# Row maxima from half sums and half differences: differences in two banks of their own, half sums from the query stage on, and six query buffers with reloads

## The chip, the cores and the metric

The kernel runs on one core of one Trainium2 chip, in one launch. The metric is the device time of that core in microseconds (us); the value compared is the median over runs. Engine names: PE is the matrix engine (TensorE), DVE is VectorE, ACT is ScalarE, POOL is GpSimd, SP is SyncE, which issues most DMAs here.

## What is computed

```python
B, S, D, H = 1, 2048, 512, 32;  Dh = D // H          # 16
# A: sliding window of 8 keys, dilated by 2, its own q, k, v for 32 heads
qkv = x @ wqkv;  logits over idx = pos - (0, 2, ..., 14);  a = softmax(...) applied to v, @ wo_a
# B: 32 query heads share one key and one value head, all 2048 keys
q = (x @ wq).reshape(B, S, H, Dh).transpose(0, 2, 1, 3);  k = x @ wk;  v = x @ wv
p = softmax(einsum("bhqd,bkd->bhqk", q, k) * Dh ** -0.5)
b = einsum("bhqk,bkd->bhqd", p, v), heads joined, @ wo_b
g = sigmoid((x * gate_w).sum(-1))
out = g * a + (1 - g) * b
```

All inputs and outputs are fp32. The weights wq and wk of B are large enough that its softmax needs the maximum of each row.

## The kernel before

**The work of B** is cut into `NU` = 32 units, each of 512 queries by 4 heads. For a unit the program does two things. First it finds the maximum of each query over all 2048 keys: matmuls with the queries as weights (`max_mm`, L321) put scores of 128 queries by 512 keys into a PSUM bank, and DVE reduces them. Such a piece, one bank of 512 columns, is called a half here; a unit has 64 of them, all units 2048 (`NF`). Two rows of the query buffer (rows 62 and 63 of each row half) then receive the shifts worked out from the maxima (`shift_a` to `shift_d`). Later come 16 exponential steps per unit, 512 in all: in each, `exp_pair` (L470, L472) puts scores of 128 keys by 512 queries into the banks `eb` twice, ACT takes the exponential of 1024 columns, and `weighted` (L480) multiplies with the values into the bank `po`.

**Maxima** are formed in three ways. `fill_pair` reduces two halves in one DVE instruction from the two-bank tile `m2` (L341); `fill_one` reduces one half from the bank `m1`, in the front from `po` too (L352). The third way takes two key blocks together: max(a, b) = (a + b) / 2 + |a - b| / 2. `half_keys` forms the half sums and half differences of the keys once (`kcd`); then `fill_diff` multiplies the queries with the half differences into both banks of `m2`, ACT writes the absolute values to SBUF (`dd`, L416), and `fill_sum` multiplies with the half sums into `m1` and `po`, where one DVE instruction adds the absolute values and takes the maximum (L426). Such a group of two differences and two sums stands for four halves. `slots` is the list of what is still to be done, in order of units.

**The order** is written out by a program that keeps a clock for each engine (`clk`, `after`, with fixed costs such as T_R, T_LAT, T_TTR) and a time at which each bank is free (`free`). In the front (about the first 280 us) `stream` puts out the projection matmuls, 64 rows at a time: one half of the array rows takes a projection matmul, and the other row half either the next one or a single matmul of the maxima. The projections are 16 query blocks (`("q", m)`, the first two ahead of the stream) and 64 blocks of A (`("a", gg, j)`), called lumps, 24 matmuls each, which alternate between `eb[0]` and `eb[1]` (L1046); after each lump ACT copies its banks out and POOL adds the two row halves. Half sums are formed at lumps `("a", 0, 4)` and `("a", 0, 6)`.

In the steps, each iteration asks `fill_ready` for a pair on `m2` and for a single on `m1`. Singles are asked for only while

```python
return 2 * max(0, 16 * (NU - 1) - 16 - s) + PER_ROW * max(0, NJ - 4 - outs) < to_go()
```

holds. Three times, `out_phase` stops the steps and projects four blocks of 128 output rows, again by `stream`, with groups of half sums beside the projection (L735). A phase begins when the maxima are fewer than `LEAD` = 3 units ahead of the steps, or at a set step. The last four output rows are spread over the last steps (`spread`). POOL works at A's window attention from the front until the last third.

**Buffers.** `qst` has eight query buffers, the last two being halves of the tile `q67`. A unit's queries are loaded once, by `stack` (four DMAs on SP: L290, L291), into the buffer that `home` gives, and stay there from the maxima to the end of the unit's steps. `stack` is called in the query stage for the first eight units and then each time a unit's steps are over. `kcd` lies in a pool of the front; it is written to scratch and read back into `q67` (`half_back`) when those two buffers are no longer used.

## Time and profile before

| | |
|---|---|
| median of 3 runs | 1503.54 us (1503.17 to 1504.63) |
| the profiled execution | 1503.16 us, its span 1501.4 us |
| mean granted TensorE clock | 0.999 of full speed |
| busy of the span | PE 1477.8 us (98%), ACT 1284.1 (86%), DVE 1188.7 (79%), POOL 1023.6 (68%) |
| DMA | 87.75 MB, mean 58 GB/s |

The span runs from the first to the last instruction of the program; the time of an execution is 1.8 us more. In a group's row stand line, engine, operation, output<-input by the program's names (the bank tiles `m2`, `m1`, `po`, `eb` show as pm, ps, po, pe; queries in the two buffers of `q67` as q), the shape and the count, then after the bar the busy time in us, the mean of one instruction in ns, and the idle time of the engine just before, with what ended it. A row of a window gives its length, then the busy time and the count on each engine, the granted clock, the share of the DMA engines and GB/s. PE counts as busy while a matmul is in flight, so a busy PE is not PE at its peak.

### The profile page before, as it was taken

Reading aid. Unit: us, or ns where it says so; the run is one execution under the profiler, and the core shown is the slowest. Engines: PE = TensorE matmul, PEld = TensorE weight load, DVE = VectorE, ACT = ScalarE, POOL = GpSimd, SP = SyncE. Lnnn points to the kernel's source line nnn. Section 1 sums busy time; section 2 is a strip of 40 time slices with the busy share of each in tenths; the row PEclk is TensorE's granted clock in tenths of the full one; section 3 lists DMA queues with packets and bytes.
Section 4 is the critical chain, followed back from the end, with each engine's and each line's share of the span. In section 5 each row is a group of like instructions: output and inputs, shape, how many; then the busy total and the mean of one; then the engine's idle time right before and its main releaser. Section 6 shows DMA issues by size and latency. Waiting matters only on the chain.

```text
span 1501.4 us, 29244 instructions
## 1 busy us (share of the span) xinstructions
PE 1477.8 (98%) x10920; PEld 706.0 (47%) x10920; DVE 1188.7 (79%) x1813; ACT 1284.1 (86%) x1668; POOL 1023.6 (68%) x1804
## 2 busy tenths in 40 slices
PE   7999999999999999999999999999999999999998
PEld 4988888533333333333363334633333373333334
DVE  5976666788888888888888888888888878888801
ACT  4558988899999999999988999899999979999885
POOL 7866987788988888888898789888888030111020
PEclk9999999999999999999999999999999999999999
DMA  6754223121120211211202112021120000000000
GB/s 219 199 150 138 78 84 123 44 83 41 55 89 6 84 58 41 70 41 41 70 27 78 46 35 75 30 69 41 41 70 11 17 31 16 2 1 2 1 1 29
DMA packets 44287, 87.75 MB, mean 58 GB/s; under 512 B 9520, under 2 KB 25952, under 8 KB 39920
## 3 DMA queue, kind: packets, MB, share of 16 engines
q1 hardware_dynamic: 36704, 46.10, 10.2%
q0 software_dynamic: 6432, 37.94, 7.6%
q8 instruction: 86, 1.41, 0.4%
q10 hardware_dynamic: 1008, 1.84, 0.4%
q14 instruction: 57, 0.47, 0.1%
HBM read 59.02 MB, written 26.30 MB: 57 GB/s over the span
## 4 chain that ended last, share of the span: by engine, by line
PE 92%; ACT 4%; DVE 1%; issue 1%; POOL 1%; DMA 1%; DVEq 0%; ACTq 0%; POOLq 0%
PE po L480 33%; PE pe L470 25%; PE pm L321 8%; PE pe L1046 8%; PE ps L321 5%; PE pe L735 4%; PE pm L406 2%; ACT dd L416 2%; PE ps L406 1%; PE pe L180 1%; ACT pexp L472 1%; PE po L406 1%; PE ps L807 1%; PE pm L807 1%; DVE dd L426 0%
## 5 line engine op out<-in xcount | busy, mean ns | idle before, releaser
L472 ACT ACTIVATE pexp<-pe 128x1024 f32<-128x1024 f32 x1021 | 987.3, 1023 | 100.7 <-PE pe L470 98.0
L341 DVE TENSOR_REDUCE mx<-pm 128x2 f32<-128x1024 f32 x508 | 620.1, 1221 | 142.9 <-PE pm L321 138.9
L480 PE MATMUL po<-pexp,vst 128*32 128x512 f32 x4096 | 545.5, 605 | 0.0
L470 PE MATMUL pe<-qst,kst 64*128 64x512 f32 x1914 | 520.3, 454 | 3.6 <-ACT pexp L472 2.2
L470 PEld LDWEIGHTS pe<-qst,kst 64*128 64x128 f32 x1914 | 213.5, 184 | 421.5 <-ACT pexp L472 409.8
L352 DVE TENSOR_REDUCE mx<-ps 128x1 f32<-128x512 f32 x453 | 307.5, 679 | 3.3 <-PE ps L321 3.3
L321 PE MATMUL pm<-kst,qst 62*128 62x512 f32 x974 | 197.6, 397 | 1.4 <-DVE mx L341 1.4
L540 POOL TENSOR_TENSOR pr<-aext 128x256 f32<-128x256 f32 x256 | 182.8, 741 | 0.3
L321 PE MATMUL ps<-kst,qst 62*128 62x512 f32 x430 | 181.0, 421 | 0.7 <-DVE mx L426 0.4
L600 POOL TENSOR_TENSOR oa<-oa,av 128x256 f32<-128x256 f32 x224 | 164.4, 734 | 15.4
L480 PEld LDWEIGHTS po<-pexp,vst 128*32 128x32 f32 x4096 | 80.5, 108 | 174.1 <-issue 166.1
L597 POOL TENSOR_TENSOR av<-aext,lg 128x256 f32<-128x256 f32 x224 | 139.7, 623 | 12.6
L321 PEld LDWEIGHTS ps<-kst,qst 62*128 62x128 f32 x430 | 78.9, 184 | 72.4 <-DVE mx L352 67.1
L416 ACT ACTIVATE dd<-pm 128x512 f32<-128x512 f32 x166 | 92.2, 609 | 21.9 <-DVE mx L426 10.9
L1046 PE MATMUL pe<-wal,xh 64*128 64x384 f32 (+1 forms) x504 | 107.8, 337 | 0.0
L1046 PE MATMUL pe<-wah,xl 64*128 64x384 f32 (+1 forms) x504 | 107.7, 338 | 0.0
L1046 PE MATMUL pe<-wah,xh 64*128 64x384 f32 (+1 forms) x504 | 107.7, 338 | 0.0
L426 DVE CUSTOM_DVE_ANT_0 dd<-ps,dd 128x512 f32<-128x512 f32 x83 | 57.4, 692 | 58.9 <-PE ps L406 26.6
L321 PEld LDWEIGHTS pm<-kst,qst 62*128 62x128 f32 x974 | 93.9, 186 | 6.0 <-DVE mx L341 2.8
L506 POOL TENSOR_TENSOR rl<-rl,gate_t 128x16 f32<-128x16 f32 x31 | 6.9, 222 | 129.1 <-DVE rl L500 128.9
L546 POOL TENSOR_TENSOR tr<-pr 128x512 f32<-128x512 f32 x64 | 81.7, 1276 | 3.8
L256 POOL TENSOR_TENSOR stage<-stage,two 128x384 f32<-128x384 f32 x64 | 65.1, 1016 | 26.2 <-ACT two L247 13.4
(223 smaller groups left out, 1897.7 us busy)
## 6 DMA issues: line engine op xcount, KB each, us to landing
aext<-ad POOLq DMA_DIRECT2D x32, 1056.0 KB, 5.4
ad<-stage SPq DMA_DIRECT2D x32, 384.0 KB
qst<-qd SPq DMA_DIRECT2D x60, 128.0 KB
xraw<-xt SPq DMA_DIRECT2D x16, 256.0 KB
qd<-qhi SPq DMA_DIRECT2D x16, 256.0 KB
qd<-qlo SPq DMA_DIRECT2D x16, 256.0 KB
qst<-qd SPq DMA_DIRECT2D x60, 64.0 KB
qst<-ml SPq DMA_DIRECT2D x216, 2.0 KB
```

The lines of the kernel that those rows point to most:

```text
L321: nc.tensor.matmul(dst, qst[home(v)[0]][b:b + 62, pr, t * P:(t + 1) * P], kst[b:b + 62, kc * 512:(kc + 1) * 512], start=True, stop=True)
L341: nc.vector.tensor_reduce(m[:, :, pr, t, kc], dst, AX.X, ALU.max)
L352: nc.vector.tensor_reduce(m[:, odd, pr, t, kc:kc + 1], dst, AX.X, ALU.max)
L416: nc.scalar.activation(dd[0][:, odd], m2[:, odd, :], AF.Abs)
L470: nc.tensor.matmul(bank[:, odd, :], kst[b:b + 64, kt * P:(kt + 1) * P], qst[home(u)[0]][b:b + 64, pr, :], start=True, stop=True)
L472: nc.scalar.activation(e, bank, AF.Exp, scale=SCALE)
L480: nc.tensor.matmul(po[32 * i:32 * i + 32, :], vst[:, kt, :], pexp[s, i // 2][:, i % 2, :], start=(kt == 0), stop=(kt == NJ - 1))
L540: nc.gpsimd.tensor_mul(pr[:, k], q, e[:, o:o + NH, AC:2 * AC])
L546: nc.gpsimd.tensor_add(nx, cur[:, :, 0:n], cur[:, :, n:2 * n])
L597: nc.gpsimd.tensor_mul(av, e[:, o:o + NH, 2 * AC:].rearrange("p j (h d) -> p j h d", d=DH), lg[:, w].unsqueeze(3).to_broadcast([P, NH, AG, ...
L600: nc.gpsimd.tensor_add(ao, ao, av)
L1046: nc.tensor.matmul(front[2 if x == last else x % 2][0][:, b, :n], l[h], r[h], start=(i == 0), stop=(i == 3 * C - 1))
```

## The change

Four things change together.

- **Banks.** The two banks of `m2` become a pool that is released and allocated anew (`banks_of`): either one tile `m2` of two banks, as before, or two tiles `hv[0]` and `hv[1]` of one bank each. While `hv` is there, `fill_diff` puts out one difference matmul at a time, as a single of `stream`, into the bank of its row half, and the two banks come free separately. Up to three sums may be open (`pend`), and each of two `dd` buffers has its own times (`until`), so the next group's differences may go ahead of this group's sums. `hv` is there from the query stage to the last lump and in each output phase; in the steps `m2` is back.
- **Half sums earlier.** `half_sel` moves to lump `("q", 3)`, and `half_keys` to `("q", 4)` and `("q", 5)`, as soon as the banks are free (`wants`). From then on, while the next slots are paired, the front takes no direct reductions. `kcd` lies in the constant pool for good, so scratch `kd` and `half_back` go.
- **Six query buffers.** `load_next` loads the unit after the one whose maxima are being done, into any buffer that `vacant` gives: an empty one, one whose unit's steps are over, or one whose maxima are done and which is not to stay. Units that are at most `STAY` = 2 ahead of the steps when loaded stay until their steps are over. The others are loaded a second time by `load_again`, one or two units ahead of their steps.
- **Shifts through scratch.** For a unit that does not stay, `shift_d` writes its shifts to scratch `sd` in place of the query buffer, and `load_again` reads them back with two DMAs on SP.

Beside these, the value and gate columns of the first 16 lumps of A leave their bank in one ACT copy in place of two, unit 1 no longer shares its order of slots with unit 0, and `ended` (no new groups at the end of a stream) is set two to three items sooner. The core of the diff (small renamings left out; of `half_keys` and `half_parts` only the places of the tiles change):

```diff
@@ -34,7 +34,7 @@
-NB = 8
+NB, STAY = 6, 2
@@ -63,19 +63,32 @@
+    kcd = cp.tile([P, 2, 2, 512], F32R, name="kcd")
+    sd = dp.tile([NU, 2, 2, 1024], F32, name="sd")
...
-    m2 = pp.tile([P, 2, 512], F32, name="pm")
...
+    m2, hv, mp = None, [], []
+    def banks_of(two):
+        nonlocal m2
+        if mp:
+            mp.pop().release()
+        mp.append(tc.alloc_tile_pool(name="pair", bufs=1, space=PSUM))
+        m2, hv[:] = None, []
+        if two:
+            hv.extend(mp[0].tile([P, 512], F32, name=f"pd{x}") for x in range(2))
+            free["d0"] = free["d1"] = free["m2"]
+        else:
+            m2 = mp[0].tile([P, 2, 512], F32, name="pm")
+            free["m2"] = max(free["m2"], free["d0"], free["d1"])
+    free = {"m2": 0.0, "m1": 0.0, "e0": 0.0, "e1": 0.0, "po": 0.0, "d0": 0.0, "d1": 0.0}
+    banks_of(False)
@@ -278,31 +290,59 @@
-    stacked, asked = [], set()
-    def stack(u):
-        qb, hg = divmod(u, NHG)
+    there, where, holds, stayed, ended_max, outs_q, now_u = {}, {}, [None] * NB, set(), set(), [1], [0]
+    def vacant():
+        for k in sorted(range(NB), key=lambda k: -1 if holds[k] is None else holds[k]):
+            w = holds[k]
+            if w is None or w < now_u[0] or w in ended_max and w not in stayed:
+                return k
+    def load(v, k):
+        holds[k], where[v] = v, k
+        qb, hg = divmod(v, NHG)
...
-            dst = qst[home(u)[0]].rearrange("p c n -> p (c n)").bitcast(F32)
+            dst = qst[k].rearrange("p c n -> p (c n)").bitcast(F32)
...
-        stacked.append(clk["pe"] + 5.0)
+    def load_next(first=False):
+        v = len(there)
+        if first or v < NU and v <= (slots[0][0] if slots else NU) + 1 and v // 2 + (2 if outs_q[0] < 15 else 0) <= outs_q[0]:
+            k = vacant()
+            if k is not None:
+                if v - now_u[0] <= STAY:
+                    stayed.add(v)
+                load(v, k)
+                there[v] = clk["pe"] + 5.0
+    def load_again(w):
+        k = vacant()
+        if w in stored and k is not None:
+            load(w, k)
+            stayed.add(w)
+            for b in range(2):
+                nc.sync.dma_start(qst[k][64 * b + 62:64 * b + 64].rearrange("x i n -> x (i n)").bitcast(F32), sd[w, b])
+            shifted.add(w)
+    stored = set()
...
-    slots = [(v, pr, t, kc) for kc in range(2) for v in range(2) for pr in range(2) for t in range(4)]
-    slots += [(v, pr, t, kc) for v in range(2) for pr in range(2) for t in range(4) for kc in range(2, 4)]
-    slots += [(v, pr, t, kc) for v in range(2, NU) for pr in range(2) for t in range(4) for kc in range(4)]
+    slots = [(0, pr, t, kc) for g in range(2) for pr in range(2) for t in range(4) for kc in (2 * g, 2 * g + 1)]
+    slots += [(v, pr, t, kc) for v in range(1, NU) for pr in range(2) for t in range(4) for kc in range(4)]
...
     def fillable():
-        return bool(half) or bool(slots) and slots[0][0] < len(stacked) and stacked[slots[0][0]] <= clk["pe"]
+        return bool(half) or bool(slots) and there.get(slots[0][0], 1e9) <= clk["pe"]
@@ -372,60 +410,81 @@
+    def diff_ready():
+        if not group and (ended or half or not hv or not paired()):
+            return False
+        odd = group[0][4] if group else 0
+        now = clk["pe"]
+        return len(pend) < len(dd) + 1 and free[f"d{odd}"] <= now + 0.1 and dd[0][1][odd] <= now + 0.9 and clk["act"] <= now + 0.7 and clk["dve"] <= now + 1.8
...
     def fill_diff():
-        v, pr, t, kc = slots.pop(0)
-        slots.pop(0)
-        for odd in range(2):
-            half_mm(m2[:, odd, :], v, pr, t, kc, 1, odd)
-        at = after("pe", 0, T_R) + T_LAT
-        dd.append(dd.pop(0))
-        for odd in range(2):
-            nc.scalar.activation(dd[0][:, odd], m2[:, odd, :], AF.Abs)
-            ready_d[odd] = after("act", at, 0.52) + 0.1
-        free["m2"] = ready_d[1]
-        pend.extend([(v, pr, t, kc, 0), (v, pr, t, kc, 1)])
+        if not group:
+            v, pr, t, kc = slots.pop(0)
+            slots.pop(0)
+            group.extend([(v, pr, t, kc, 0), (v, pr, t, kc, 1)])
+        v, pr, t, kc, odd = group.pop(0)
+        dst, until = dd[0]
+        if odd:
+            dd.append(dd.pop(0))
+        half_mm(hv[odd], v, pr, t, kc, 1, odd)
+        at = clk["pe"] + T_R + T_LAT
+        nc.scalar.activation(dst[:, odd], hv[odd], AF.Abs)
+        at = after("act", max(at, until[odd]), 0.52) + 0.1
+        free[f"d{odd}"] = at
+        pend.append((v, pr, t, kc, odd, at, dst, until))
+    def sum_ready():
+        return pend and free[("m1", "po")[pend[0][4]]] <= clk["pe"] + 0.1 and pend[0][5] <= clk["pe"] + 0.4
...
     def fill_sum():
-        v, pr, t, kc, odd = pend.pop(0)
+        v, pr, t, kc, odd, ready, d, until = pend.pop(0)
...
-        nc.vector.tensor_tensor_reduce(dd[0][:, odd], dst, dd[0][:, odd], 1.0, -FMAX, ALU.add, ALU.max, m[:, odd, pr, t, kc:kc + 1])
-        free[key] = after("dve", max(clk["pe"] + T_R + T_LAT, ready_d[odd]), T_TTR) + 0.08
+        nc.vector.tensor_tensor_reduce(d[:, odd], dst, d[:, odd], 1.0, -FMAX, ALU.add, ALU.max, m[:, odd, pr, t, kc:kc + 1])
+        free[key] = until[odd] = after("dve", max(clk["pe"] + T_R + T_LAT, ready), T_TTR) + 0.08
...
+    def finish_groups():
+        while group or pend:
+            if group:
+                odd = group[0][4]
+                clk["pe"] = max(clk["pe"], free[f"d{odd}"])
+                fill_diff()
+            else:
+                odd, at = pend[0][4:6]
+                clk["pe"] = max(clk["pe"], free[("m1", "po")[odd]], at - 0.3)
+                fill_sum()
+            clk["pe"] += T_R
@@ -454,10 +513,13 @@
     def shift_d(v, ml, k):
...
-        dst = qst[home(v)[0]][64 * b + 62:64 * b + 64].rearrange("x i (t q) -> x i t q", t=4).bitcast(F32)
+        if v in stayed:
+            dst = qst[where[v]][64 * b + 62:64 * b + 64].rearrange("x i (t q) -> x i t q", t=4).bitcast(F32)
+        else:
+            dst = sd[v, b].rearrange("x (i t q) -> x i t q", i=2, t=4)
...
-            shifted.add(v)
+            (shifted if v in stayed else stored).add(v)
@@ -683,20 +745,24 @@
-    def stream(seq, mm, done, pooled):
+    def stream(seq, mm, done, pooled, held=()):
...
         while min(at) < len(seq):
...
-            if pend:
-                if free[("m1", "po")[pend[0][4]]] <= clk["pe"] + 0.1 and ready_d[pend[0][4]] <= clk["pe"] + 0.4:
-                    single, odd = fill_sum, pend[0][4]
-            elif paired() and not half:
+            if wants and all(free[k] <= clk["pe"] + 0.1 for k in (("m1", "po") if wants[0] else ("m2",))):
+                half_keys(wants.pop(0))
+            if sum_ready():
+                single, odd = fill_sum, pend[0][4]
+            elif hv and (group or paired() and not half):
+                if diff_ready():
+                    single, odd = fill_diff, group[0][4] if group else 0
+            elif 1 in wants:
...
-            elif fillable() and free["m1"] <= clk["pe"] + 0.1:
+            elif fillable() and not pend and free["m1"] <= clk["pe"] + 0.1:
...
-            elif pooled and fillable() and free["po"] <= clk["pe"] + 0.1:
+            elif pooled and fillable() and not pend and free["po"] <= clk["pe"] + 0.1:
@@ -704,16 +770,11 @@
-                elif at[b] < len(seq):
+                elif at[b] < len(seq) and not (seq[at[b]] in held and told < at[b]):
...
-            if ended:
-                pass
-            elif paired():
-                if not half and not pend and max(free["m2"], clk["dve"] - 1.2) <= clk["pe"] + 0.1:
-                    fill_diff()
-            elif slots and fillable() and free["m2"] <= clk["pe"] + 0.1:
+            if m2 is not None and not ended and 0 not in wants and slots and fillable() and free["m2"] <= clk["pe"] + 0.1:
@@ -756,17 +817,14 @@
-            formed.update((0, 1))
+            banks_of(True)
...
-        formed.clear()
+        finish_groups()
+        if whole_unit:
+            banks_of(False)
@@ -1034,10 +1092,16 @@
-            if lump == ("a", 0, 3):
+                dd.append((pm[0].tile([P, 2, 512], F32, name="dd", bufs=1), [0.0, 0.0]))
+            if lump == ("q", 3):
...
-            elif lump in (("a", 0, 4), ("a", 0, 6)):
-                half_keys(1 if lump[2] == 4 else 0)
+                dd.append((p1.tile([P, 2, 512], F32, name="dd", bufs=1), [0.0, 0.0]))
+            elif lump in (("q", 4), ("q", 5)):
+                wants.append(5 - lump[1])
+            elif x == last:
+                finish_groups()
+                banks_of(False)
+                front[2] = (m2, "m2")
@@ -1094,13 +1158,17 @@
-        if s == 16 * NB + 4:
-            half_back()
-        if len(stacked) < NU and s > 16 * (home(len(stacked))[1] + 1):
-            stack(len(stacked))
+        now_u[0] = u
+        if kt > 2:
+            for w in (u + 1, u + 2):
+                if w < NU and w in ended_max and w not in stayed:
+                    load_again(w)
+        load_next()
...
+                if u in stored:
+                    load_again(u)
```

90 lines of the change are left out of this document (38 added, 52 removed).

## The prediction

> **What bounds the kernel now.** I read the page first, then busy time by stage, the timeline of a few steps, and last the grouped instructions of the front (everything before the exponential steps, 0 to 282 us) and of what follows.
>
> ```profile
> span 1501.4 us, 29244 instructions
> PE 92%; ACT 4%; DVE 1%; issue 1%; POOL 1%; DMA 1%; DVEq 0%; ACTq 0%; POOLq 0%
> ```
>
> The chain that ended last is 92% PE, so a change pays only where it shortens PE's queue or lets a PE stall go. The stages differ:
>
> ```profile
> core 0: us, PE busy (x) PEld busy (x) DVE busy (x) ACT busy (x) POOL busy (x), PEclk, DMA share, GB/s
> 40.00:90.00 50.00, 50.00 (x449) 47.36 (x447) 49.93 (x67) 25.77 (x42) 42.65 (x43) 1.00 0.71 197
> 110.00:270.00 160.00, 156.38 (x1558) 140.58 (x1556) 105.64 (x328) 134.48 (x315) 128.86 (x205) 1.00 0.34 104
> 500.00:600.00 100.00, 100.00 (x699) 35.83 (x699) 86.88 (x105) 92.49 (x100) 87.07 (x171) 1.00 0.15 51
> 758.00:791.00 33.00, 32.52 (x288) 24.07 (x286) 27.68 (x80) 25.80 (x51) 28.48 (x50) 1.00 0.08 28
> ```
>
> The query projection (40:90) has a full VectorE and a half idle ScalarE; the projection of A (110:270) and an output phase (758:791) have room on both; the steps (500:600) have PE full and ScalarE at 92%. All work of this change is maxima: 2048 "halves" (128 queries by 512 keys). Where they are done today:
>
> ```profile
> L426 DVE CUSTOM_DVE_ANT_0 dd<-ps,dd 128x512 f32<-128x512 f32 x83 | 57.4, 692 | 58.9 <-PE ps L406 26.6 <-ACT dd L416 24.9 <-ACT mx L315 5.5
> L341 DVE TENSOR_REDUCE mx<-pm 128x2 f32<-128x1024 f32 x28 | 33.8, 1209 | 5.2 <-PE pm L321 5.2
> L352 DVE TENSOR_REDUCE mx<-ps 128x1 f32<-128x512 f32 x27 | 18.2, 674 | 2.8 <-PE ps L321 2.8
> L352 DVE TENSOR_REDUCE mx<-po 128x1 f32<-128x512 f32 x26 | 17.5, 674 | 0.0
> ...
> L341 DVE TENSOR_REDUCE mx<-pm 128x2 f32<-128x1024 f32 x480 | 586.3, 1221 | 137.7 <-PE pm L321 133.8
> L352 DVE TENSOR_REDUCE mx<-ps 128x1 f32<-128x512 f32 x426 | 289.3, 679 | 0.5 <-PE ps L321 0.5
> L426 DVE CUSTOM_DVE_ANT_0 pexp<-ps,pexp 128x512 f32<-128x512 f32 x53 | 36.7, 692 | 16.8 <-PE ps L406 12.0 <-ACT pexp L416 3.4 <-PE pe L735 1.2
> ```
>
> The first four rows are the front, the last three the rest. A group of half sums and differences is four halves (one L426 on each of ps and po, two halves each), so the front does 83 x 4 + 28 x 2 + 53 = 441, the steps 480 x 2 + 426, the output phases 53 x 4 = 212. The sum is 2039; a few records are missing.
>
> What one half costs PE is different in a step and in the front. A step with only a pair, then one with a pair and a single:
>
> ```profile
> 549.81 1.07 PE L480 MATMUL po<-pexp,vst 128*32 128x512 f32 x8
> 551.43 3.81 ACT L472 ACTIVATE pexp<-pe 128x1024 f32<-128x1024 f32 x4 [0.23 <-PE pe L470]
> 551.71 1.06 PE L480 MATMUL po<-pexp,vst 128*32 128x512 f32 x8
> 553.28 0.39 PE L321 MATMUL ps<-kst,qst 62*128 62x512 f32 x1
> 553.87 1.06 PE L480 MATMUL po<-pexp,vst 128*32 128x512 f32 x8
> ```
>
> ```profile
> 500.00:600.00 100.00, 50.08 (x376) 7.39 (x376) 1.00 0.15 51
> 500.00:600.00 100.00, 27.77 (x41) 1.00 0.15 51
> ```
>
> The second fence holds the windows of L480 (376 / 8 = 47 steps in 100 us) and of L352 (41 singles). The step from 549.81 to 551.71 had no single: 1.90 us. If the six others cost that, a step with a single costs (100 - 6 x 1.90) / 41 = 2.16 us. Nearly every step carries one, because the emitter asks for singles while more halves are left than pairs alone can do by step 480 (20 credited for each output row to come).
>
> In the front a half shares the array with the projection, in the other row half:
>
> ```profile
> 274.26 0.34 PE L1046 MATMUL pe<-wah,xl 64*128 64x384 f32 x2
> 274.44 0.34 PE L1046 MATMUL pe<-wah,xh 64*128 64x384 f32 x2
> 274.98 0.39 PE L406 MATMUL ps<-kcd,q 62*128 62x512 f32 x1
> 275.15 0.33 PE L1046 MATMUL pe<-wal,xh 64*128 64x384 f32 x1
> 275.21 0.34 PE L1046 MATMUL pe<-wah,xh 64*128 64x384 f32 x1
> ```
>
> Pairs of projection matmuls follow each other every 0.18 us (274.26, 274.44); the half at 274.98 holds its rows until 275.21, 0.23 us, while the other rows go on. A half costs PE 0.23 / 2 = 0.115 us there, against 2.16 - 1.90 = 0.26 us as a single.
>
> **The change part by part.**
>
> *Singles that leave the steps.* Taken away from one step in eight, a single is worth 0.26 us. Taken away from many in a row it is worth less, for ScalarE becomes the limit: its share of the 500:600 row is 92.49 / 47 = 1.97 us a step (saving 0.19); four exponentials back to back took 3.81 us, so two take 1.91 and with 0.03 for the rest 1.94 (saving 0.22). I take 0.21, ends 0.19 and 0.26. By the Trainium skill ("ScalarE: Activation LUTs", What ACT_TABLE_LOAD costs) an ACTIVATE takes 186 ns + 0.833 ns an element and back-to-back ones overlap by about 93 ns: an estimate of 0.95 us for 1024, in agreement with 3.81 / 4; by it the saving would be 0.24 and the time below some 4 us lower.
>
> *Front, query stage.* The half sums start some 50 us sooner, and the direct reductions there end. Between 40 and 90 us ScalarE has 24 us free; at 1.11 us a group (next fence) that is 22 groups, 88 halves, and I take 80. VectorE, full today, gives 86 in that stretch (its rows there: 21 pairs, 44 singles). So nothing is won: -6. The stretch around 90 to 110 us, where today the half sums are being formed, goes on at full rate: 7 lumps at 7 halves for 16 now, +33.
>
> *Front, projection of A.* Today's limit is the order difference, two |d|, two sums, then the next difference:
>
> ```profile
> L416 ACT ACTIVATE dd<-pm 128x512 f32<-128x512 f32 x156 | 86.7, 609 | 20.2 <-DVE mx L426 10.9 <-PE pm L406 9.1
> L246 ACT ACTIVATE stage<-pe 128x384 f32<-128x384 f32 x52 | 25.5, 490 | 4.9 <-PE pe L1046 2.2 <-DMA ad<-stage 1.6 <-PE po L406 0.3
> L426 DVE CUSTOM_DVE_ANT_0 dd<-ps,dd 128x512 f32<-128x512 f32 x78 | 54.0, 692 | 53.6 <-ACT dd L416 24.2 <-PE ps L406 22.0 <-ACT mx L315 5.5
> PEld pm L406 <- ACT dd L416: 13.0, 36, 1.6
> ```
>
> From 110 to 270 us: 52 lumps (L246 runs once in each), 3.08 us a lump, 78 groups, 1.5 a lump. ScalarE spends 86.7 / 78 = 1.11 us a group and (134.48 - 86.7) / 52 = 0.92 on the rest of a lump; VectorE 2 x 0.69 = 1.38 a group. PE waited 13.0 us for |d| to free the shared bank. Two banks, each freed by its own |d|, and two dd buffers let differences run ahead. The emitter charges ScalarE 0.8 + 1.04 g and PE 0.18 an iteration, 2.16 + 0.36 g a lump, and puts out a difference while its ScalarE clock is at most 0.7 us ahead: that closes at g = 2.0, less for the first 16 lumps (1.0 in place of 0.8), for gate copies and exponentials of A. I take 1.8, ends 1.5 and 2.0. On the chip PE then needs 12 x 0.175 + 7.2 x 0.115 = 2.93, ScalarE 0.92 + 1.8 x 1.11 = 2.92, VectorE 2.6: all under 3.08, but close together, so waits remain. Halves: 56 lumps x 0.3 x 4 = +67. Together the front gains 94. PE pays 94 x 0.115 = 10.8 us; I let half of the 13.0 us go and add 2 us for the two changes of banks and the tail of open groups before the last lump (0 to 4): front **+6** us, ends -5 and +20. What is late next is ScalarE: behind a difference that waits for its bank stand, on PE, the projection matmuls, and behind |d| on ScalarE the copies that free the projection's banks.
>
> *Output phases.* From one step's last matmul to the next:
>
> ```profile
> 756.39 1.06 PE L480 MATMUL po<-pexp,vst 128*32 128x512 f32 x8
> 793.41 1.06 PE L480 MATMUL po<-pexp,vst 128*32 128x512 f32 x8
> ```
>
> In such a phase of 37 us there are 53 / 3 = 18 groups. ScalarE has 33 - 25.8 = 7 us free, VectorE 5.3: four more groups (ends 0 and 7), 16 halves for 1.84 us of PE, and two bank changes with the wait for the last reader, between 0 and 1.4 us (|d| 0.61, then L426 0.69), taken as 0.7. Three phases: **+7.5** us, 48 halves.
>
> *Loads and shifts.* Six buffers for eight, units from the third on loaded twice, their shifts through scratch and back.
>
> ```profile
> 51.75 0.59 SPq L290 DMA_DIRECT2D qst<-qd  x1
> 53.62 0.58 SPq L291 DMA_DIRECT2D qst<-qd  x1
> SPq L458 <- POOL ml L444: 269.2, 18, 52.0
> ```
>
> A load is four issues from 51.75 to 54.2 us, 2.4 us of SP; a second load with its two shift reads about 3.6 us, some 29 times, 104 us of a queue that spends most of the span waiting. The load of a maxima unit is put out when the unit before it begins: 64 halves, some 10 lumps or 30 us ahead in the front, 22 steps or 47 us in the steps. That hides it; I cost it at nothing. On SP it can stand behind shift writes that wait for GpSimd (up to 52.0 us in the row); those waits end with the same GpSimd work as now, and mostly show SP idle, not late. If the cover went, each load would cost PE 2.4 us and a landing: 0 to 30 us over the whole kernel. Two ScalarE copies of 0.2 us become one in 16 lumps: off the path. DMA share 0.15 in the steps rises little.
>
> **Sum.** 94 + 48 = 142 singles x 0.21 = -29.8; front +6; phases +7.5: -16. From the profiled execution's own 1503.16 us (span 1501.4) that is 1487; the median of the runs shown is 0.4 us higher, so **1488**.
>
> **Rivals.**
>
> *B, no waits left.* ScalarE overlaps fully and 2.0 groups fit: PE 2.10 + 8 x 0.115 = 3.02 a lump, the front 4 us shorter, 187 halves gone from the steps at 0.23 = -43, phases +7.5: 1464. For it: every engine has room on average. Against: the waits of the last fence come from real times that differ from the charged ones, and those stay.
>
> *C, slower: the front becomes bound by emptying banks.* The emitter issues 2.0 groups a lump on charges that are too low (0.18 an iteration that holds a 0.23 us half; no charge for splits). Then a |d| follows its own difference without overlap, at 609 ns: ScalarE 0.92 + 4 x 0.609 = 3.36 a lump, and with today's PE wait of 13.0 / 78 = 0.17 a group, 3.70. Over 64 lumps +40; 187 halves save 39; phases +7.5: 1511. It decides from 3.57 us a lump on ((39 - 7.5) / 64 above 3.08). For it: ScalarE is already 84% busy from 110 to 270. Against: it has 25 us idle there and PE waits only 13. The Trainium skill ("TensorEngine Tiling (Array Packing)", PSUM Bottleneck) says that row tiling speeds up the array but not the emptying of PSUM, which may become the limit; by that rule C is what happens, and today's row (13.0 us in 160) bears it out only in part.
>
> *D, it hardly does what it says.* The emitter's own conditions (ScalarE 0.7 us, VectorE 1.8 us, open sums below three) hold the groups at 1.5 a lump and the phases at 18: the +33 and -6 halves stay, 27 x 0.21 = -6 against +3 in the front and +2 in the phases: 1503.
>
> **How the numbers follow.** The forecast has 0.62, B 0.12, C 0.17, D 0.09. About 0.2% (3 us) is what a measurement of this kernel can tell from no change. The forecast's own bounds (saving 0.19 to 0.26, front -5 to +20, groups 1.5 to 2.0) give 1470 to 1500. The range 1467 to 1508 adds the near side of B and D and the loads' price, and leaves out most of C. Faster is the forecast but a thin edge and B: 0.73. Same is D and that edge: 0.08. Slower is C and a small part of the rest: 0.19.
>
> **What would show it.** Right: L426 counts in the front near 105 to 125 a bank in place of 83; singles (L352 on ps) after the front near 280 to 290 in place of 426, gone in the second half of the steps, where steps last 1.92 to 1.97 us; the first L480 within 275 to 300 us; 20 to 24 groups a phase. Wrong: lumps above 3.5 us with PE waiting for ACT dd (C); single-free steps at 2.1 us; PE waiting for a load of qst or for shifts; L426 counts as now (D).

## The result: slower by 1.1%, and the profile after

The changed kernel took 1521.29 us (median of 4 runs, 1520.03 to 1522.22), the kernel before 1504.09 beside it (1503.17 to 1506.95): a ratio of 1.0111, 95% interval 1.0093 to 1.0128. The forecast was 1488, its range 1467 to 1508. The profiled execution took 1522.22 us. The head of its page, and the head of the chain that ended last:

```profile
span 1520.4 us, 29896 instructions
PE 1488.4 (98%) x10920; PEld 705.4 (46%) x10920; DVE 1145.3 (75%) x1847; ACT 1337.6 (88%) x1745; POOL 1013.4 (67%) x1793
PE 91%; ACT 4%; DVE 2%; DMA 1%; issue 1%; POOL 1%; SPq 0%; DVEq 0%; ACTq 0%; POOLq 0%
```

PE carries the chain as before, over 19.0 us more of span. The maxima moved as intended, which the VectorE groups show (front first, then the rest):

```profile
L473 DVE CUSTOM_DVE_ANT_0 dd<-ps,dd 128x512 f32<-128x512 f32 x122 | 84.2, 690 | 44.3 <-PE ps L440 19.0 <-ACT dd L460 13.3 <-PE pe L1110 4.4
L382 DVE TENSOR_REDUCE mx<-pm 128x2 f32<-128x1024 f32 x6 | 7.3, 1218 | 5.2 <-PE pm L361 5.2
L393 DVE TENSOR_REDUCE mx<-ps 128x1 f32<-128x512 f32 x8 | 5.5, 682 | 1.6 <-PE pe L1110 1.5
...
L382 DVE TENSOR_REDUCE mx<-pm 128x2 f32<-128x1024 f32 x469 | 572.6, 1221 | 168.6 <-PE pm L361 164.7
L393 DVE TENSOR_REDUCE mx<-ps 128x1 f32<-128x512 f32 x356 | 242.0, 680 | 1.4 <-PE ps L361 1.4
```

122 groups in the front where there were 83, and 356 singles after it where there were 426. (L440, L460 and L473 are the difference matmul, the |d| and the half sum, before L406, L416 and L426; L361, L382 and L393 are the score matmul, the pair and the single, before L321, L341 and L352.) Yet the front lasted longer than these groups save later. Cut at the first matmul of P times V, at step 480 and at the three output phases:

| us | before | after | difference |
|---|---|---|---|
| front, to the first PV matmul | 279.6 | 302.8 | +23.2 |
| halves done in it | 440 | 515 | +75 |
| three output phases | 109.6 | 114.4 | +4.8 |
| other steps to 480 | 1017.2 | 1010.1 | -7.1 |
| singles in the steps | 431 | 357 | -74 |
| after step 480 | 95.0 | 93.1 | -1.9 |

The loss is the front, and the gain of the steps is a quarter of the forecast's 29.8 us. In the windows of the changed kernel (query stage, projection of A, steps, output phase):

```profile
45.00:85.00 40.00, 39.08 (x321) 29.87 (x318) 23.78 (x62) 32.30 (x55) 31.42 (x30) 1.00 0.55 147
200.00:290.00 90.00, 90.00 (x892) 80.79 (x890) 72.80 (x221) 85.28 (x179) 75.55 (x117) 1.00 0.36 112
500.00:600.00 100.00, 100.00 (x701) 35.66 (x698) 87.24 (x107) 92.53 (x101) 83.73 (x154) 1.00 0.22 70
883.00:918.00 35.00, 34.98 (x304) 25.20 (x302) 30.20 (x87) 30.91 (x56) 33.00 (x50) 1.00 0.16 56
```

and the projection of A before, in the same columns:

```profile
180.00:270.00 90.00, 87.42 (x868) 77.82 (x868) 60.72 (x190) 74.57 (x164) 76.16 (x116) 1.00 0.31 96
```

PE's waits in the projection are gone (90.00 busy of 90, before 87.42), and ScalarE rose from 74.57 / 90 = 83% to 85.28 / 90 = 95%. Undisturbed lumps last 90 / 29 = 3.1 us, little more than before (90 / 30 = 3.0), with 53 / 29 = 1.83 groups in place of 46 / 30 = 1.53. So the front lost its time mainly elsewhere. Two stops of PE stand in its timeline; matmuls of 384 columns at 160.10 took 0.34 us, and then:

```profile
96.78 0.79 PE L440 MATMUL pd<-kcd,qst 62*128 62x512 f32 x1 [2.86 <-ACT dd L460]
...
160.10 0.34 PE L1110 MATMUL pe<-wah,xh 64*128 64x384 f32 x1
165.57 0.79 PE L440 MATMUL pd<-kcd,qst 62*128 62x512 f32 x1 [4.54 <-ACT dd L460]
167.55 0.52 PE L1110 MATMUL pe<-wah,xh 64*128 64x384 f32 x2
171.38 0.34 PE L1110 MATMUL pe<-wal,xh 64*128 64x384 f32 x1
```

The stops cost more than themselves, as the clock column of the windows around the second shows:

```profile
161.00:165.00 4.00, 0.04 (x2) 0.00 (x0) 0.00 (x0) 0.84 (x3) 0.00 (x0) 0.91 0.37 106
165.00:169.00 4.00, 3.43 (x20) 3.43 (x22) 2.10 (x6) 3.11 (x8) 1.70 (x2) 0.50 0.30 98
169.00:172.00 3.00, 3.00 (x26) 3.00 (x24) 1.02 (x3) 2.00 (x5) 2.54 (x3) 0.65 0.00 0
172.00:176.00 4.00, 4.00 (x40) 3.45 (x38) 3.04 (x11) 3.72 (x9) 2.90 (x4) 1.00 0.46 147
```

After the stop PE ran at a granted clock of 0.50 until 171.1 (the 0.65 of 169:172 is 2.1 us at half speed). Half the speed for 5.5 us loses 2.75, so the stop cost about 4.54 + 2.75 = 7.3 us; the first, with half speed from 96.8 to 102.8, cost 2.86 + 3.0 = 5.9. Both figures are estimates: they suppose that PE set the pace while its clock was low. The Trainium skill ("TensorE: Matmul & The Clock Gate", Part 1, The HAM clock gate) says that PE's clock goes to half after an idle window of about 3.4 us and comes back after as long a busy one. The trace agrees on the half, but not on an idle window: the clock fell at 96.0, 2.1 us after PE's last matmul, and the first stop was only 2.86 us long; it came back after 6.8 us both times.

What stopped PE at 161? Its difference waited for a bank, the bank for |d|, and |d| stood on ScalarE behind a copy (L258) that waited 4.83 us for its buffer, whose contents a store on SP had yet to take. SP's timeline and its wait:

```profile
157.72 0.40 SPq L275 DMA_DIRECT2D ad<-stage  x1
158.16 4.88 SPq L520 DMA_DIRECT2D qst<-ml  x7
164.12 14.82 SPq L275 DMA_DIRECT2D ad<-stage  x3
```

```profile
SPq L520 <- POOL ml L503: 8.3, 1, 8.3
```

L520 writes the shifts of a unit. SP had stood 8.3 us at the first (156.99) until GpSimd had formed ml; the store at 157.72 came right behind it, and the copy went on at 164.16, when it had landed. In the first stop |d| waited for its own place instead: the second dd buffer lies where the queries had been, and had to wait for a DMA that still read them (3.4 us).

### The profile page after: what moved, and what is told of

It is laid out like the page before. It is cut to its first block, busy times and chain, and to the rows that moved or that the text cites. A ratio compares the mean times of both kernels' runs of the same rounds, so it can differ in the third digit from the quotient of the medians.

```text
span 1520.4 us, 29896 instructions
## 1 busy us (share of the span) xinstructions
PE 1488.4 (98%) x10920; PEld 705.4 (46%) x10920; DVE 1145.3 (75%) x1847; ACT 1337.6 (88%) x1745; POOL 1013.4 (67%) x1793
## 4 chain that ended last, share of the span: by engine, by line
PE 91%; ACT 4%; DVE 2%; DMA 1%; issue 1%; POOL 1%; SPq 0%; DVEq 0%; ACTq 0%; POOLq 0%
PE po L542 32%; PE pe L532 24%; PE pe L1110 9%; PE pm L361 7%; PE ps L361 4%; PE pe L796 4%; PE pd L440 3%; PE ps L440 2%; PE po L440 2%; ACT pexp L534 2%; PE ps L865 1%; PE pm L865 1%; PE pe L193 1%; DMA ad<-stage 1%; DMA xraw<-xt 1%
## 5 line engine op out<-in xcount | busy, mean ns | idle before, releaser
L382 DVE TENSOR_REDUCE mx<-pm 128x2 f32<-128x1024 f32 x475 | 579.9, 1221 | 173.8 <-PE pm L361 169.9
L532 PE MATMUL pe<-qst,kst 64*128 64x512 f32 x2042 | 543.3, 458 | 4.4 <-ACT pexp L534 4.3
L393 DVE TENSOR_REDUCE mx<-ps 128x1 f32<-128x512 f32 x364 | 247.5, 680 | 3.0 <-PE pe L1110 1.5
L361 PE MATMUL pm<-kst,qst 62*128 62x512 f32 x953 | 191.8, 397 | 1.8 <-DVE mx L382 1.3
L662 POOL TENSOR_TENSOR oa<-oa,av 128x256 f32<-128x256 f32 x224 | 164.0, 732 | 14.7
L460 ACT ACTIVATE dd<-pd 128x512 f32<-128x512 f32 x244 | 140.5, 601 | 22.2 <-PE pd L440 9.3
L440 PE MATMUL pd<-kcd,qst 62*128 62x512 f32 x362 | 146.4, 406 | 9.7 <-ACT dd L460 9.6
L361 PE MATMUL ps<-kst,qst 62*128 62x512 f32 x364 | 153.7, 422 | 0.3 <-DVE mx L393 0.3
L1110 PE MATMUL pe<-wah,xh 64*128 64x384 f32 (+1 forms) x504 | 129.5, 352 | 0.3 <-ACT two L220 0.3
L1110 PE MATMUL pe<-wah,xl 64*128 64x384 f32 (+1 forms) x504 | 127.0, 347 | 0.0
L473 DVE CUSTOM_DVE_ANT_0 dd<-ps,dd 128x512 f32<-128x512 f32 x122 | 84.2, 690 | 44.3 <-PE ps L440 19.0
L473 DVE CUSTOM_DVE_ANT_0 dd<-po,dd 128x512 f32<-128x512 f32 x122 | 84.2, 690 | 32.0 <-PE po L440 13.6
L361 PEld LDWEIGHTS ps<-kst,qst 62*128 62x128 f32 x364 | 66.8, 184 | 62.6 <-DVE mx L393 58.2
L361 PEld LDWEIGHTS pm<-kst,qst 62*128 62x128 f32 x953 | 90.7, 186 | 5.8 <-DVE mx L382 3.5
```

Source lines behind the costliest of these rows:

```text
L361: nc.tensor.matmul(dst, qst[where[v]][b:b + 62, pr, t * P:(t + 1) * P], kst[b:b + 62, kc * 512:(kc + 1) * 512], start=True, stop=True)
L382: nc.vector.tensor_reduce(m[:, :, pr, t, kc], dst, AX.X, ALU.max)
L393: nc.vector.tensor_reduce(m[:, odd, pr, t, kc:kc + 1], dst, AX.X, ALU.max)
L440: nc.tensor.matmul(dst, qst[where[v]][b:b + 62, pr, t * P:(t + 1) * P], kcd[b:b + 62, kc // 2, x, :], start=True, stop=True)
L460: nc.scalar.activation(dst[:, odd], hv[odd], AF.Abs)
L473: nc.vector.tensor_tensor_reduce(d[:, odd], dst, d[:, odd], 1.0, -FMAX, ALU.add, ALU.max, m[:, odd, pr, t, kc:kc + 1])
```

## The experiments

Theories. R: every half moved into the front costs more there than a single is worth in the steps, by waits that come from running ahead. S: the extra loads and shifts stand in SP's order and stop PE. E: the early half sums and the second dd place cost the query stage. U: the steps give back less per single than was reckoned. (In the expectations, theory 1 is E, with 1b for the second dd place alone; 2 is S; 3 is U; and 4 is the two prices measured in the runs before.)

**Half sums formed later** (theory E).

```
-            if lump == ("q", 3):
+            if lump == ("a", 0, 3):
...
-            elif lump in (("q", 4), ("q", 5)):
-                wants.append(5 - lump[1])
+            elif lump in (("a", 0, 4), ("a", 0, 6)):
+                wants.append(1 if lump[2] == 4 else 0)
```

> The changed kernel, but with the half sums formed at lumps (a,0,3), (a,0,4) and (a,0,6) as before, so that the query stage reduces directly on VectorE. Theory 1 (most of the longer front comes from the query stage: ScalarE holds the query copies and |d| there, and the last queries come out late): last copy of the front 10 to 13 us sooner (from 302 to about 290), as many halves in the front within 20, total about 1509. Rival (the loss is in the projection of A, where groups were added): front shorter by under 4 us, total 1517 to 1521.

Measured: 1507.42 us, 1.0024 of before (1.0014 to 1.0034). The first PV comes at 282.3, 20.5 us sooner, with 505 halves, and both stops are gone, though E has a reason for the first only: in the front nearly twice the gain that was expected. The shift writes stand where they stood, and in the front SP waits for ml as long as in the changed kernel (that one first):

```profile
SPq L520 <- POOL ml L503: 28.0, 6, 8.3
SPq L520 <- POOL ml L503: 30.0, 7, 8.2
```

So SP's wait stops PE only together with the early half sums. The steps are 8.1 us longer and the phases 3.0 shorter: 39 singles more, and three steps of 2.8 to 3.3 us. In two of these PE waits for the load of a unit, in the one at 452 us for ScalarE, which copies output weights (L94) first.

**Shift writes issued later in the front** (theory S).

```
-                tasks.append((clk["pe"] + 0.8 * k, shift_d, (v, ml, k)))
+                tasks.append((clk["pe"] + 12.0 + 0.8 * k, shift_d, (v, ml, k)))
```

> The changed kernel, but the shift writes of the front are put out 12 us later on the emitter's clock, so that SP does not stand before GpSimd's ml with a store of A behind it. Theory 2: the one stop of 4.5 us at 160 us (ScalarE waits for the store, PE for ScalarE) goes, total about 1516. Rival: the store is late for another reason or the stop moves to another place, total unchanged at 1521.

Measured: 1512.46 us, 1.0058 (1.0043 to 1.0073), front 293.2: 9.6 us won by the order of SP alone, nearly twice what was expected. Stores now go ahead of the writes:

```profile
149.26 14.31 SPq L275 DMA_DIRECT2D ad<-stage  x3
163.62 3.35 SPq L520 DMA_DIRECT2D qst<-ml  x5
```

The stop at 161 is gone (7.3 us), and the first came out shorter, 2.11 us, with half speed from 96.5 to 99.9 (3.8 in place of 5.9): 9.4 of the 9.6.

**One group at a time** (theory R): a difference is put out only when the sums of the group before are.

```
-        if not group and (ended or half or not hv or not paired()):
+        if not group and (pend or ended or half or not hv or not paired()):
```

> The changed kernel, but a new group starts only when no sum of the last one is open, as before; banks, half sums and buffers stay. Theory (the groups that running ahead adds cost the front about as much as they save in steps): 40 to 60 fewer groups, front 4 to 8 us shorter, 40 to 60 more singles in the steps at about 0.15 us, total 1518 to 1523. Rival (running ahead overloads ScalarE and is what costs): total below 1512. Rival (running ahead is the gain and something else costs more): total above 1526.

Measured: 1553.87 us, 1.0334 (1.0319 to 1.035), against the theory and on the side of the second rival. The front ended at 278.4, but with 417 halves, fewer than before, and the steps could not make up for them. Units came due with maxima missing, and PE waited for VectorE to reduce them; the windows of one such place:

```profile
1189.00:1193.00 4.00, 2.10 (x8) 0.67 (x8) 4.00 (x4) 0.00 (x0) 0.00 (x0) 0.81 0.00 0
1193.00:1197.00 4.00, 2.83 (x9) 1.07 (x7) 4.00 (x5) 0.50 (x1) 0.00 (x0) 0.50 0.00 0
1197.00:1201.00 4.00, 3.12 (x12) 0.99 (x14) 1.42 (x2) 1.55 (x2) 0.00 (x0) 0.50 0.00 0
```

VectorE is full, ScalarE empty, and PE's clock falls to 0.50. Four such steps lasted 11.3 to 14.0 us each; one of 9.8 us at 452 is of another kind, ScalarE waiting for output weights. So running ahead pays for the halves that the steps can't do; whether it pays for the others is seen only with the front's other faults mended (below).

**Singles spread evenly** (theory U): `single_now` adds up the share of singles that a step still needs and lets one go when the sum reaches 1, in place of all steps until they run out.

```
-                if not later_rows and (kt or not s) and singles(s):
+                if not later_rows and (kt or not s) and single_now(s):
```

> The changed kernel, but the steps' singles are spread evenly over the steps that are left, in place of one in every step until none is needed. Theory 3 (ScalarE alone limits a run of steps without singles at 2.01 us, while a lone one lasts 1.90): the 120 steps without a single fall from 1.97 to about 1.90 us, total 6 to 9 us lower, 1512 to 1515. Rival (a lone short step only takes back what its neighbours lost): total 1519 to 1522.

A miss: 1529.98 us, 1.0176 (1.0159 to 1.0192). Steps without a single did cost 1.924 us, as U has it, but the maxima came late, the phases had fewer groups (17, 16 and 21), two steps took 9.9 and 5.2 us, and PE stopped 6.8 us at 408.6 behind SP: eight shift writes were ahead of the load of the output weights that ScalarE was waiting for.

```profile
405.10 3.54 SPq L520 DMA_DIRECT2D sd<-ml  x8
408.74 0.84 SPq L684 DMA_DIRECT2D os<-wo_a  x2
```

**Both mended: late half sums and later shift writes**, in the steps too (8 us).

```
-            if pe:
-                shift_d(v, ml, k)
-            else:
-                tasks.append((clk["pe"] + 0.8 * k, shift_d, (v, ml, k)))
+            tasks.append((clk["pe"] + (8.0 if pe else 12.0 + 0.8 * k), shift_d, (v, ml, k)))
```

> Half sums formed late, as in late_keys, and the shift writes put out later on the emitter's clock both in the front (12 us) and in the steps (8 us), so that SP never stands long before ml. Theory 2 carried on (what late_keys still loses in the steps is loads and stores that stand behind shift writes on SP): the steps of 2.8, 3.3 and 3.0 us at 79, 275 and 323 go, total 1502 to 1504. Rival (the second loads themselves, or six buffers, cost it): total unchanged at 1506 to 1508.

Measured: 1505.04 us, 0.9999 (0.999 to 1.0008): all that the change lost is back, and nothing won. (The kernel before took 1505.22 us beside it; the expected 1502 to 1504 is missed by 1 us.) Front 282.6 with 505 halves, as with late half sums alone: the later writes win nothing in this front, only 2.3 us in the steps. Of the three long steps the one at 452 us stays (2.81).

**Second dd place taken later** (on top of the later shift writes in the front): the pool's second tile is made at the fourth lump of A.

```
+            if lump == ("a", 0, 3):
                 dd.append((pm[0].tile([P, 2, 512], F32, name="dd", bufs=1), [0.0, 0.0]))
```

> The changed kernel with the front's shift writes 12 us later (as shift_delay, 1512.5) and the second dd buffer taken only from lump (a,0,3) on, since it lies where the last query parts are still being written out. Theory 1b (the stop of 2.1 us at 93 us comes from that buffer): total 1509 to 1511. Rival (ScalarE's backlog after the query stage makes it): 1512 to 1513, the stop stays.

The front gained as reckoned, 293.2 to 289.2, but the whole took 1516.79 us, 1.0076 (1.0061 to 1.0092), more than without it. The steps lost it again: one took 4.34 us and one 6.61, the first while ScalarE waited for output weights, the second while PE waited for the load of a unit. The waits of the second, and SP ahead of them (before these writes SP was at stores of output rows until 1114.94):

```profile
PEld pm L361 <- DMA qst<-qd: 4.1, 2, 2.3
PE pm L361 <- DMA qst<-qd: 3.5, 2, 2.0
```

```profile
1115.03 3.62 SPq L520 DMA_DIRECT2D sd<-ml  x8
1118.69 0.54 SPq L310 DMA_DIRECT2D qst<-qd  x1
```

**No singles in the steps at all** (theory U). Left out: a quarter of the maxima of units 8 to 31 (two of eight query tiles), so that pairs alone suffice.

```
-                if not later_rows and (kt or not s) and singles(s):
+                if not later_rows and (kt or not s) and s < 0:
```

> The changed kernel without any single in the steps; for units 8 to 31 a quarter of the maxima is left out (two of eight query tiles), so that pairs alone suffice. It measures the step that has a pair and no single when all steps are such. Theory 3 (ScalarE's two exponentials and a stop of 0.18 us in every second step): mean 2.00 to 2.02 us. Rival (the forecast's floor): 1.94 to 1.97.

One run, 1490.25 us. The windows of its PV matmuls alone:

```profile
500.00:800.00 300.00, 157.71 (x1188) 23.28 (x1184) 1.00 0.19 59
```

1188 / 8 = 148.5 steps in 300 us, 2.02 each, as expected. Over all 477 steps to step 480 the mean is 2.044 with five long ones (2.9 to 7.4 us, two of them stops of PE) and 2.017 without these. A step with a single costs 2.169 in the changed kernel, 2.164 without its long ones, so taking the single from every step gains 0.125 to 0.15 us, not 0.21.

**Both mended, one group at a time** (theory R again): the diff of both mended with the condition `pend or` of one group at a time.

> As late_delay, but a group starts only when no sum is open, as before the change. Theory (running ahead is worth its PE time only as far as the steps still pay for singles): 50 to 70 fewer halves in the front, front 8 to 14 us shorter, total within 3 us of late_delay. Rival (running ahead overloads ScalarE): 5 us or more below late_delay. Rival (running ahead is a clear gain): 5 us or more above.

Measured: 1527.23 us, 1.0148 (1.0134 to 1.0161), 22 us above the kernel that runs ahead, where the theory had 3. Front 264.9 with 429 halves, and again three steps of 11.2, 14.0 and 14.0 us before the last units (and one of 7.9 at 1163). Set beside the kernel that runs ahead with both mended, in the groups of the front (that one first):

```profile
L473 DVE CUSTOM_DVE_ANT_0 dd<-ps,dd 128x512 f32<-128x512 f32 x96 | 66.2, 690 | 23.1 <-PE ps L440 10.7 <-ACT dd L460 5.5 <-PE pe L1107 2.3
```

```profile
L473 DVE CUSTOM_DVE_ANT_0 dd<-ps,dd 128x512 f32<-128x512 f32 x77 | 53.3, 692 | 33.8 <-PE ps L440 20.2 <-ACT dd L460 5.1 <-ACT mx L355 3.6
```

19 groups, 76 halves, for 282.6 - 264.9 = 17.7 us: 0.233 us a half. Beside the kernel before (279.6, 440 halves) this front is 14.7 us shorter; 11 halves of that are 2.6, so 12.1 us come from the rest of the change. Most of it are the waits that a bank of its own removes: over lumps 8 to 60 PE and its weight loads waited 14.1 us for |d| to free the shared bank in the kernel before, and 0.4 us here.

Where the 0.233 goes can be read in these two kernels. Over the same 52 lumps, with 292 halves here, a lump lasts 2.84 us; the projection takes 12 x 0.175 = 2.1 of them, which leaves at most 0.13 for each of the 5.6 halves. So a half that comes on top costs more than its rows, by waits of the weight loads for banks (the kernel that runs ahead first, 104.6:268.2, then this one, 104.6:252.1):

```profile
PEld ps L440 <- DVE mx L473: 6.2, 20, 1.0
PEld pd L440 <- ACT dd L460: 3.6, 14, 0.4
PEld po L440 <- DVE mx L473: 2.4, 9, 0.3
```

```profile
PEld ps L440 <- DVE mx L473: 1.2, 2, 1.0
PEld pd L440 <- ACT dd L460: 0.4, 2, 0.2
PEld po L440 <- DVE mx L473: 0.4, 1, 0.4
```

10.2 us more of them stand beside 68 halves more, and VectorE, which empties the banks of the sums, ended more of them than ScalarE.

**Running ahead in the later part of the front only**, from the third or fourth row of A, with both mended. If a half costs 0.233 in the front and brings 0.125 to 0.15, the best is the fewest that still avoids the stops.

```
-        if not group and (ended or half or not hv or not paired()):
+        if not group and (pend and not ahead or ended or half or not hv or not paired()):
...
+            if lump == ("a", 2, 0) or x == last:
+                ahead.append(1)
```

> late_delay, but in the front a group may start while sums are open only from lump (a,2,0) on, half way through the projection of A; in the output phases as in late_delay. Theory 4 (a half that running ahead adds to the front costs 0.23 us there and saves 0.125 us as a single in the steps, as long as the steps can still finish them): about 38 fewer halves in the front, front 9 us shorter (273 to 275), 30 more singles, total 1499 to 1502, below before. Rival (the steps run short of halves and stop, as in late_serial): 1508 or more. Rival (the forecast's prices, 0.115 in the front and 0.21 in the steps): 1508 to 1510.

> As ahead_half, but from lump (a,3,0) on, the last quarter of the projection. Theory 4: some 55 to 60 fewer halves in the front than late_delay, front 268 to 270, total 1497 to 1501, if the steps can still finish them without a stop. Rival (too few halves: stops of 11 to 14 us before a unit's steps): 1510 or more.

Measured: 1500.26 us, 0.9977 (0.9968 to 0.9986), front 276.5 with 477 halves; and 1499.46 us, 0.9975 (0.9965 to 0.9985), 271.1 with 456. Both totals are as expected, the fronts 1 to 2 us longer; the two kernels can't be told apart. The fronts give the price twice more: (282.6 - 276.5) / 28 = 0.22 and 5.4 / 21 = 0.26. But the way was another than theory 4 has it: in the first of the two the singles in the steps did not rise by 30 (391, with both mended 396). The 28 halves went to six more groups in the phases, which took 4.2 us longer, and to four more pairs. So these totals don't test the price of a single.

**All of it early, but mended**: the changed kernel with the later shift writes in front and steps and the later dd place.

> The changed kernel with early half sums and all mends of the queue: shift writes later in front and steps, second dd buffer from lump (a,0,3) on. It stands against late_delay, which differs only in the half sums being late. Theory 1 (the early half sums themselves cost the query stage time, ScalarE being full there): front 288 to 290 against 282.6, total 1508 to 1511 against 1505. Rival (only the queue's stops made the early half sums bad): front within 3 us, total within 2 us of late_delay.

Measured: 1515.13 us, 1.0078 (1.0064 to 1.0091), above the expected. The front was right (289.4), four long steps of 2.8 to 4.6 us remain. Against the same with late half sums the front is 6.8 us longer for 10 halves more: 4.5 us beyond their price, at a full clock and without a stop. The loss lies in the query stage: the copy after the first lump of A starts at 90.4 us with 80 halves done, with late half sums at 84.4 with 91; behind it 21 halves more cost 0.8 us.

**The best of them, with the next unit's load also asked for in the output phases** (on the kernel that runs ahead from the third row).

```
                 run_tasks()
+                load_next()
```

> As ahead_half, and the next unit's queries are also asked for inside the output phases, where the changed kernel asks for none. Theory (a phase does more than one unit's halves, so that the first maxima after it wait for a load and some groups are lost): 2 to 4 more groups in the three phases, no step over 2.6 us after them, total 1 to 3 us below ahead_half. Rival (the loads are there in time): unchanged.

Measured: 1498.53 us, 0.9967 (0.9955 to 0.998), 1.7 us below the same without it. The signs named for it did not come: 56 groups in the phases where there were 60, and steps of 2.9 to 3.2 us after them. The phases are 4.5 us shorter and the steps 2.9 longer; why that gains is not shown. It beats the kernel before by 0.3% and the changed one by about 1.4%:

```profile
span 1497.0 us, 29665 instructions
PE 1475.7 (99%) x10920; PEld 705.6 (47%) x10920; DVE 1181.7 (79%) x1821; ACT 1298.7 (87%) x1672; POOL 1015.6 (68%) x1798
```

## Why the prediction was wrong

Right were the group counts (105 to 125 a bank forecast, 122 came; 1.8 groups a lump, 1.83 came) and the end of PE's waits for the shared bank (6.5 us reckoned; 12.1 came with all else that the change does). The phases were half right: +7.5 us for twelve groups more were reckoned, +4.8 for six came (21, 18 and 20). The first PV matmul came at 302.8, outside the 275 to 300 named. One reading was wrong without harm: no records are missing from the 2039 halves, the other nine stand in small groups that the rows leave out (seven singles on pm, a pair on pe). The total failed in five steps.

*Price of a half in the front: 0.115 us reckoned, 0.233 measured.* The step counted PE's rows only. The rest are waits for banks that ScalarE and VectorE empty, as the two kernels above show; ScalarE, at 1.11 / 4 = 0.28 us a half and 95% busy, has little free time left, but how much is its share and how much VectorE's is not shown. 75 halves cost 17.5 us, not 8.6. "All under 3.08, but close together" was read as room for 94 halves at the price of their rows, where it meant that the waits would grow with every half.

*Price of a single: 0.21 reckoned, 0.125 to 0.15 measured.* The floor of 1.95 for steps without singles came from a lone step (1.90) and from ScalarE's sum. One after the other, such steps take 1.90 and 2.13 in turn:

```profile
1380.46 3.83 ACT L534 ACTIVATE pexp<-pe 128x1024 f32<-128x1024 f32 x4 [0.18 <-PE pe L532]
1380.76 1.06 PE L542 MATMUL po<-pexp,vst 128*32 128x512 f32 x8
1382.89 1.07 PE L542 MATMUL po<-pexp,vst 128*32 128x512 f32 x8
1384.49 3.85 ACT L534 ACTIVATE pexp<-pe 128x1024 f32<-128x1024 f32 x4 [0.19 <-PE pe L532]
1384.79 1.07 PE L542 MATMUL po<-pexp,vst 128*32 128x512 f32 x8
```

Four exponentials run on end, then ScalarE waits 0.18 us for scores: the next two score matmuls wait for a bank that ScalarE empties, with the PV matmuls between. So 4.03 us for two steps, where the sum of ScalarE's work had given 3.9. The Trainium skill ("ScalarE: Activation LUTs", What ACT_TABLE_LOAD costs) would make an ACTIVATE of 1024 elements 0.95 us, an estimate; the trace agrees (3.83 / 4), but neither holds the wait in between. The kernel itself says the same: cut at their PV matmuls, steps without a single went from 64 at 1.917 to 120 at 1.972, so the added 56 cost (120 x 1.972 - 64 x 1.917) / 56 = 2.03, against 2.166 with one.

*142 singles gone: 74.* Front and phases gave 75 + 24 = 99 halves, where 142 were reckoned, and 24 of these took the place of 12 pairs, which cost a step little (in the kernel without singles 28 steps without a pair too lasted 1.98 us, the others 2.02). 61 fewer steps with a single at 0.13 are 7.9 us; -7.1 came.

*Loads and shifts at nothing: 9.6 us in the front, beside early half sums.* The step read SP's long wait for ml as idleness ("mostly show SP idle, not late"). It is that only while nothing behind it is due; here stores of A stood behind it, and through the staging buffer ScalarE and PE. The working asked whether the load comes in time and not what stands behind the write. The price is not one of the order alone: with the half sums late the same order cost the front nothing (282.3 against 282.6). In the steps of the experiments it made single ones up to 9.9 us long.

*Query stage at no time: +6.8 and +4.0.* The early half sums cost 6.8 us, 4.5 of them beyond the price of their 10 halves, and the stage did 11 halves less, not 6. By what mechanism is open: PE is busy 39.08 of 40 us there, 35.00 of 35 before. The second dd place cost 4.0 (3.8 by stop and half clock).

Together, in the front: 75 x 0.233 = 17.5, less 12.1, with 4.5, 4.0 and 9.6: 23.5 where 23.2 was measured. That the sum closes proves nothing, for its terms are the differences of neighbours in one row of kernels from before to after. Taken in another order they differ: late half sums alone bring back 20.5 of the 23.2. With the phases (+4.8), the steps (-7.1) and the end (-1.9) that is the +19.0. Rival C had the direction and ScalarE as the engine, but not the way: lumps stayed at 3.1 to 3.2 us, well under its 3.57, and 18.1 of the front's 23.5 us were stops, a slow clock and the query stage. Of the theories of the experiments U held in size; S and E held in direction and brought nearly twice what was expected in the front, for late half sums also removed the stop that S names, and later writes shortened the one that E names. R's price held, but both kernels with one group at a time became slower, since their steps ran short of halves.

## What to carry to other kernels

The price of work moved beside other work is not the rows that it takes on one engine (0.115 us a half here) but that and the waits it adds for what the other engines must empty (0.233); and the worth of work taken away is measured by taking it from all places in a row, since a lone one shows more (0.26 us against 0.125 to 0.15). For each DMA put into an engine's queue ask what stands behind it while it waits, and through which buffer that reaches the engine that sets the time: issuing such writes 12 us later was worth over half a per cent here. What such a wait costs depends on the rest: once the half sums were late, it cost the front nothing.

## What the runs showed of the hardware

A short stop of PE brings the clock down, and for a fixed time. In the clock records of all fourteen runs, leaving out each run's end, the stretches at half speed last 3.41 us or two, three or four times that, and all changes of a run lie on one grid of 3.41 us. After a stop of 2.11 us (one of 0.79 a few us before) one such stretch followed; 2.86 and 4.54 us were followed by two each. After a stop of 1.7 us in the kernel before the clock stayed at 1.00. The rows give the stretch of the grid that holds the start of the 2.11 us and the one after it, then the stretch with most of the 1.7 us:

```profile
93.11:96.52 3.41, 1.30 (x13) 0.75 (x10) 0.70 (x2) 1.57 (x5) 0.18 (x2) 1.00 0.29 75
96.52:99.93 3.41, 3.12 (x18) 2.97 (x18) 2.01 (x5) 2.52 (x6) 1.75 (x4) 0.50 0.46 130
```

```profile
92.61:96.02 3.41, 2.21 (x14) 1.55 (x16) 1.97 (x4) 1.84 (x6) 1.86 (x4) 1.00 0.15 27
```

PE was busy 1.30 of 3.41 us and the next stretch was at half, or 2.21 and it was not. Over all runs each stretch at full speed in which PE was busy at most 0.41 of the time was followed by half speed, and none with 0.57 or more; between them both occur. So where on this grid a stop falls counts too: stops of 1.93 and 1.99 us in other runs left the clock at 1.00. By the estimates above, stops of 2.11 to 4.54 us cost 1.6 to 2.1 times their length. The Trainium skill ("TensorE: Matmul & The Clock Gate", Why this matters for your kernels) asks for no gaps above about 3 us; here 2.11 was enough, and the measurement decides.
